# FNet mixing plus MLP on one core: the column transform taken for pairs of row blocks, with seven block products for eight on four fifths of its columns

## The chip, the cores and the metric

The kernel runs on one core of one Trainium2 chip. The metric is the device time of one execution in microseconds, taken as the median of several runs.

## What is computed

The reference, cut to what matters (S = 2048 rows, D = 640 columns, F = 1536 hidden units, all float32):

```python
xn = layernorm(x)                                   # without scale and shift, eps 1e-5
a  = einsum("bsd,ed->bse", xn, dft_hid_re)          # wr in the kernel
b  = einsum("bsd,ed->bse", xn, dft_hid_im)          # wi
y  = einsum("ts,bse->bte", dft_seq_re, a) - einsum("ts,bse->bte", dft_seq_im, b)   # cr, ci
h  = gelu(einsum("bsd,df->bsf", xn, w1) + b1)       # tanh form
return x + y + einsum("bsf,fd->bsd", h, w2) + b2
```

The four transform matrices are inputs like any other; nothing is assumed of them. The kernel takes y in the other order: first the sequence transform, u = cr xn and v = -ci xn, then the column transform, y = u wr' + v wi'.

## The kernel before

TensorE multiplies in float32r. To keep float32 accuracy every operand is held as two forms, a high part (a float32r copy, made on ScalarE, L147) and a low part (what the copy left out, a subtraction on VectorE, L148). `split` makes both. A product of two operands is three matmuls of 128 x 128 by 128 x 512: high by high, high by low, low by high (`product`, L259 to L261).

**First half, the MLP.** Four row blocks of 512 rows (t = 0 to 3), each with 12 steps (i = 0 to 11) over chunks of 128 hidden units. At step i TensorE computes `hidden` for the step after next (15 matmuls), ScalarE takes its gelu and the high form, VectorE the low form (`gelu`, into `hs`), and then `output` multiplies the `hs` made two steps ago into five PSUM banks (15 matmuls). `background(t, i)` runs ahead of that in the program, so its instructions stand ahead of the step's gelu on ScalarE, VectorE and SyncE. It prepares the next row block's layer norm: at i = 4 (t = 1, 2; at t = 0 two steps later) the scaled rows go to DRAM in 16 transfers (`xs`), four transfers bring them back in another order (`load_z`), and at t = 1 three more load rows of x. It also prepares the forms of wr and wi in t = 1 and 2: `load_w` brings a column chunk (`wraw`), `prep_w` turns it on VectorE, splits it and stores the two forms to DRAM (`wts`), one of the ten chunks at each odd i. In t = 3 the operands of the sequence transform are built.

**Second half, the transforms.** `blocks` lists eight stages, four row blocks for each half of the rows summed over; the second half has the order 3, 0, 1, 2. The sequence transform of a stage is done with seven block products for eight: `windows` gives seven products (w) with two entries each (u = 0, 1), 216 matmuls in all, into the PSUM banks X, Y, Z (two each), US and VS. `form(n + 3)` makes the moving operand of the entry after next but one, in one of three buffers `as`, so that ScalarE's copy waits until TensorE has finished the buffer's old entry. `beside` lists for each entry what stands on the other engines beside it: turns of loaded pieces of cr and ci (`turn`), sums of them (`f3`, `f5`, `f6`, `f7`) and gathering of finished banks into `sums` (`gather`). The sums of the first half of the rows wait in DRAM (`parts1`, `parts2`).

Behind each of the last four stages stands the column transform of that row block: ten chunks (five of wr, five of wi) by five output blocks by three matmuls, 150 in all. The weights' forms come from DRAM through three buffers (`load_ws`, `ws`), the sums are split as moving operands (`split_uv`, `uv`), and the result is turned on VectorE, added to the residual and MLP rows (`add_block`) and stored (`store`).

The order on each engine is that of the program (a manual schedule). All loads and stores go through SyncE's queue, but the last stage's stores, of which ScalarE's queue takes half. Transfers wait in that queue for whatever stands ahead of them.

## Time and profile before

| | |
|---|---|
| time, median of 3 runs | 875.88 us (875.66 to 876.95) |
| the profiled execution's own time | 875.63 us |
| its span, first to last instruction | 873.9 us |
| granted TensorE clock, mean | 0.998 |
| TensorE busy | 866.0 us, 3814 matmuls |
| VectorE busy | 560.1 us |
| ScalarE busy | 303.8 us |
| DMA | 149.70 MB, mean 171 GB/s |

In the lines of the profile L12 is line 12 of the kernel. PE is TensorE, PEld its weight load, DVE VectorE, ACT ScalarE, SP SyncE; SPq and ACTq are transfers issued by SyncE and ScalarE. A timeline line has start, duration, engine, source line, operation, output<-input, and in brackets how long the engine was idle before and what ended that. A group's line has its busy time and mean in ns, and then idle time before it. A window's line has the length, the busy time of PE, PEld, DVE, ACT and POOL with instructions in brackets, the granted clock, the DMA share and GB/s.

### The profile page before, as it was taken

Reading aid. Unit: us, or ns where it says so; the run is one execution under the profiler, and the core shown is the slowest. Engines: PE = TensorE matmul, PEld = TensorE weight load, DVE = VectorE, ACT = ScalarE, POOL = GpSimd, SP = SyncE. Lnnn points to the kernel's source line nnn. Section 1 sums busy time; section 2 is a strip of 40 time slices with the busy share of each in tenths; the row PEclk is TensorE's granted clock in tenths of the full one; section 3 lists DMA queues with packets and bytes.
Section 4 is the critical chain, followed back from the end, with each engine's and each line's share of the span. In section 5 each row is a group of like instructions: output and inputs, shape, how many; then the busy total and the mean of one; then the engine's idle time right before and its main releaser. Section 6 shows DMA issues by size and latency. Waiting matters only on the chain.

```text
span 873.9 us, 10010 instructions
## 1 busy us (share of the span) xinstructions
PE 866.0 (99%) x3814; PEld 715.5 (82%) x3814; DVE 560.1 (64%) x700; ACT 303.8 (35%) x409; POOL 21.0 (2%) x22
## 2 busy tenths in 40 slices
PE   9999999999999999999999999999999999999997
PEld 7888888888888888878888888888888888888886
DVE  6554542535243778989888888884687379737713
ACT  5454432334233655433434343331133113302310
POOL 0000300030003000000000000000000000000000
PEclk9999999999999999999999999999999999999999
DMA  6746368535736967959544499628773959247603
GB/s 180 225 133 171 76 165 205 132 98 139 165 91 172 365 269 136 203 115 227 120 148 110 134 268 268 204 49 254 193 237 90 268 160 267 86 162 265 240 0 61
DMA packets 166527, 149.70 MB, mean 171 GB/s; under 512 B 44240, under 2 KB 145104, under 8 KB 165200
## 3 DMA queue, kind: packets, MB, share of 16 engines
q1 hardware_dynamic: 160528, 147.10, 61.7%
q10 hardware_dynamic: 5952, 1.97, 0.9%
q8 instruction: 30, 0.49, 0.2%
q14 instruction: 17, 0.14, 0.1%
HBM read 111.29 MB, written 37.75 MB: 171 GB/s over the span
## 4 chain that ended last, share of the span: by engine, by line
PE 98%; DVE 1%; ACT 0%; issue 0%; DVEq 0%
PE banks L259 26%; PE banks L260 26%; PE banks L261 26%; PE banks L277 19%; PE banks L523 1%; PE banks L544 0%; DVE as L148 0%; DVE v L421 0%; DVE u L421 0%; ACT as L147 0%; DVE yo L421 0%; DVE yt_last L987 0%; ACT xt L147 0%; DVE zeros L514 0%; DVE r L398 0%
## 5 line engine op out<-in xcount | busy, mean ns | idle before, releaser
L147 ACT ACTIVATE as<-r 128x1024 fp32r<-128x1024 f32 x80 | 85.0, 1063 | 212.5 <-PE banks L261 187.7
L259 PE MATMUL banks<-as,xab 128*128 128x512 f32 x352 | 136.9, 389 | 0.0
L260 PE MATMUL banks<-as,xab 128*128 128x512 f32 x352 | 136.9, 389 | 0.0
L261 PE MATMUL banks<-as,xab 128*128 128x512 f32 x352 | 136.9, 389 | 0.0
L148 DVE TENSOR_TENSOR as<-r,as 128x1024 fp32r<-128x1024 f32 x80 | 97.2, 1216 | 43.3 <-ACT as L147 43.2
L292 DVE TENSOR_TENSOR hs<-ab,hs 128x512 fp32r<-128x512 f32 x48 | 36.5, 760 | 109.3 <-ACT hs L290 109.3
L277 PE MATMUL banks<-xt,xab 128*128 128x512 f32 x420 | 99.2, 390 | 0.2 <-ACT xt L147 0.2
L277 PEld LDWEIGHTS banks<-xt,xab 128*128 128x128 f32 x420 | 78.5, 188 | 17.2 <-ACT xt L147 1.3
L259 PE MATMUL banks<-as,xc 128*128 128x512 f32 x224 | 87.3, 390 | 0.4 <-DVE v L421 0.4
L261 PE MATMUL banks<-as,xc 128*128 128x512 f32 x224 | 87.2, 389 | 0.0
L260 PE MATMUL banks<-as,xc 128*128 128x512 f32 x224 | 87.1, 389 | 0.0
L259 PEld LDWEIGHTS banks<-as,xab 128*128 128x128 f32 x352 | 66.1, 188 | 13.7
L261 PEld LDWEIGHTS banks<-as,xab 128*128 128x128 f32 x352 | 66.1, 188 | 13.7
L260 PEld LDWEIGHTS banks<-as,xab 128*128 128x128 f32 x352 | 66.1, 188 | 13.7
L286 ACT ACTIVATE ab<-banks,b1c 128x512 f32<-128x512 f32 x48 | 33.0, 687 | 115.9 <-PE banks L277 115.7
L259 PE MATMUL banks<-uv,ws 128*128 128x512 f32 x165 | 64.3, 389 | 0.0
L260 PE MATMUL banks<-uv,ws 128*128 128x512 f32 x165 | 64.2, 389 | 0.0
L261 PE MATMUL banks<-uv,ws 128*128 128x512 f32 x165 | 64.2, 389 | 0.0
L147 ACT ACTIVATE as<-rt 128x1024 fp32r<-128x1024 f32 x32 | 34.0, 1062 | 70.5 <-PE banks L261 59.8
L277 PE MATMUL banks<-xt,as 128*128 128x512 f32 x240 | 57.0, 389 | 0.0
L277 PEld LDWEIGHTS banks<-xt,as 128*128 128x128 f32 x240 | 45.1, 188 | 9.3
L259 PEld LDWEIGHTS banks<-as,xc 128*128 128x128 f32 x224 | 42.0, 188 | 9.5 <-DVE v L421 0.8
(131 smaller groups left out, 1334.9 us busy)
## 6 DMA issues: line engine op xcount, KB each, us to landing
ws<-wts SPq DMA_DIRECT2D x33, 640.0 KB, 5.5
raw<-in_A_dft_seq_re_dram SPq DMA_DIRECT2D x64, 256.0 KB, 5.8
raw<-in_A_dft_seq_im_dram SPq DMA_DIRECT2D x64, 256.0 KB, 5.3
wts<-wst SPq DMA_DIRECT2D x10, 640.0 KB, 3.2
xs<-x SPq DMA_DIRECT2D x64, 80.0 KB, 1.8
xo<-in_A_x_dram SPq DMA_DIRECT2D x16, 320.0 KB, 6.4
forms_ab<-xab SPq DMA_DIRECT2D x4, 1280.0 KB, 5.8
x<-in_A_x_dram SPq DMA_DIRECT2D x14, 320.0 KB, 6.0
```

The costliest lines, as they stand in the source:

```text
L147: nc.scalar.activation(h, s, AF.Copy)
L148: nc.vector.tensor_tensor(l, s, h.bitcast(F32), op=ALU.subtract)
L259: nc.tensor.matmul(acc, wh, mh, start=first, stop=False, skip_group_check=goes_on)
L260: nc.tensor.matmul(acc, wh, ml, start=False, stop=False, skip_group_check=goes_on)
L261: nc.tensor.matmul(acc, wl, mh, start=False, stop=last, skip_group_check=goes_on)
L277: nc.tensor.matmul(acc, W1[i][:, a, j * P : (j + 1) * P], XT[j][:, b], start=n == 0, stop=n == len(steps) - 1)
L286: nc.scalar.activation(a, acc, AF.Gelu_apprx_tanh, bias=b1c[:, i : i + 1])
L292: nc.vector.tensor_tensor(hs[:, 1], a, hs[:, 0].bitcast(F32), op=ALU.subtract)
L523: nc.tensor.matmul(wacc, warm[:, :P], warm, start=True, stop=True)
```

## The change

The column transform is done for two row blocks at once. The stages of the second half of the rows are taken as two pairs (blocks 3 and 0, then 1 and 2): sequence transform of the first (`s`), of the second (`s`), then one column transform for both (`y`). Over a pair, (u, v) of two blocks is a 2 by 2 array of blocks, and wr and wi by two pairs of output blocks another; their product is formed with seven block products for eight. The fifth output block (every chunk of the fifth 32 columns of a quarter) is outside this array; it rides as a third column on four of the seven products. So the products have widths of 3, 3, 3, 2, 2, 2, 3 blocks of 128 (`GWIDE`), each over five chunks.

The sums of wr and wi that this needs are made in t = 1 and 2 of the MLP half: `prep_w(s)` takes a chunk j of both matrices in four steps (k = 0 to 3), turns them (`turn_w`), adds and subtracts, and `put_w` splits and stores seven forms (`wits`) through two buffers `wst`. The sums of the row blocks (t1 to t4 below) are made on VectorE beside the matmuls; to hold two blocks, `sums` has two sets. The operands of the `y` entries go through the same three `as` buffers as those of `s` (three entries for each product, of two, two and one chunks); the weights' forms come through five places in the first pair and nineteen in the second (`open_g`, `load_g`). The `v` and `v1` sums of the first block of a pair are gathered at its last entry. In the second pair finished columns are stored as they come, half of the transfers from ScalarE's queue.

The diff, cut to its core:

```diff
-    wts = dram.tile([2 * ND, P, 2, D], F32, name="wts")
...
+    GWIDE = (3, 3, 3, 2, 2, 2, 3)
+    wits = [dram.tile([ND, P, 2, n * P], F32, name=f"wit{w}") for w, n in enumerate(GWIDE)]
...
+    def turn_w(m, j):
...
+        nc.vector.transpose(
+            t.rearrange("p (c q i) -> p q c i", q=Q, i=B),
+            A.pop(("wraw", m)).rearrange("p (q c) i -> p q c i", q=Q),
+        )
...
+    def put_w(w, j, main, odd=None, negative=False):
+        n = GWIDE[w] * P
+        t = A["w"].tile([P, 2, 3 * P], F32R, tag="wst", bufs=2, name=f"wst{w}_{j}")
+        split(t[:, 0, : 2 * P], t[:, 1, : 2 * P], main)
+        if odd is not None and not negative:
+            split(t[:, 0, 2 * P :], t[:, 1, 2 * P :], odd)
+        elif odd is not None:
+            h, l = t[:, 0, 2 * P :], t[:, 1, 2 * P :]
+            nc.scalar.activation(h, odd, AF.Copy, scale=-1.0)
+            nc.vector.scalar_tensor_tensor(l, odd, -1.0, h.bitcast(F32), op0=ALU.mult, op1=ALU.subtract)
+        nc.sync.dma_start(wits[w][j], t[:, :, :n].bitcast(F32))
+    def prep_w(s):
+        if s == 0:
+            load_w(0, 0)
+            load_w(1, 0)
+        j, k = divmod(s - 1, 4)
+        if s == 0 or j >= ND:
+            return
+        if k == 0:
+            turn_w(0, j)
+            turn_w(1, j)
+            if j + 1 < ND:
+                load_w(0, j + 1)
+                load_w(1, j + 1)
+        (r1, r2, r4), (i1, i2, i4) = (
+            (A["wt", m][:, : 2 * P], A["wt", m][:, 2 * P : 4 * P], A["wt", m][:, 4 * P :]) for m in range(2)
+        )
+        if k == 1:
+            put_w(0, j, r1, r4)
+            put_w(1, j, i1, i4)
+            add(r4, r4, i4)
+        if k == 2:
+            put_w(6, j, i2, i4, True)
+            add(i2, i2, r2)
+            put_w(2, j, i2, r4)
+            add(r2, r1, r2, ALU.subtract)
+        if k == 3:
+            add(r1, i2, r1, ALU.subtract)
+            put_w(3, j, r1)
+            add(i1, i1, r1, ALU.subtract)
+            put_w(4, j, i1)
+            put_w(5, j, r2)
...
-    windows = [(h, t, w) for h, t in blocks for w in range(NW)]
+    stages = []
+    for k, blk in enumerate(blocks):
+        stages.append(("s", blk))
+        if k >= NT and (k - NT) % 2:
+            stages.append(("y", (blocks[k - 1][1], blk[1])))
+    entries = [(*st, w, u) for st in stages for w in range(NW) for u in range(2 if st[0] == "s" else 3)]
...
+    KU, KV = ("u1", "u2", "u"), ("v1", "v2", "v")
+    MOV = ((KU, 0), (KV, 0), (KU, 1), (KU, 1), (KV, 1), (KU, 0), (KV, 0))
...
     def form(n):
-        if n >= 2 * len(windows):
+        if n >= len(entries):
             return
-        src = held(SRC[n // 2 % NW], n % 2)
+        kind, what, w, u = entries[n]
         a = A["as"][:, n % 3]
-        split(a[:, 0], a[:, 1], src)
-    def add(dst, a, b, op=ALU.add):
-        nc.vector.tensor_tensor(dst, a, b, op=op)
+        if kind == "s":
+            split(a[:, 0], a[:, 1], held(SRC[w], u))
+        else:
+            names, which = MOV[w]
+            src = sums[what[which], names[u]]
+            if u < 2:
+                split(a[:, 0], a[:, 1], src)
+            else:
+                split(a[:, 0, 0], a[:, 1, 0], src)
...
-            if i < 2 * ND:
-                if i == 0:
-                    load_w(m, 0)
-                if i % 2 == 1:
-                    prep_w(m, i // 2)
-                elif i // 2 + 1 < ND:
-                    load_w(m, i // 2 + 1)
+            prep_w((t - 1) * NF + i)
...
+    sets = {(0, t): int(t < NT - 1) for t in range(NT)}
+    sets.update({blk: (0, 1, 1, 0)[p] for p, blk in enumerate(blocks[NT:])})
...
+    def new_sum(h, t, k):
+        shape = (P, 2, TB) if k in PAIRS else (P, TB)
+        sums[t, k] = fr_tile(shape, f"{k}_{sets[h, t]}", f"{k}_{h}_{t}")
+        return sums[t, k]
...
+        ahead = p == 2
+        direct = h == 0 or p in (0, 2)
+        second = p in (1, 3)
+        def t1(k):
+            if not second:
+                return lambda: None
+            ua, ub = sums[blocks[b - 1][1], KU[k]], sums[t, KU[k]]
+            return lambda: add(ub, ub, ua, ALU.subtract)
...
-                4: [uv(0)] if h else [],
+                4: [t1(0)] if second else [],
...
+                6: [t1(2)] if second else [],
...
+                12: [t1(1)] if second else [],
...
+            if second and n == 3:
+                A["g", b] = [A["ws"][:, k] for k in range(3)]
+            if second and 3 <= n < 6:
+                post.append(lambda: load_g(b, n - 3))
...
+            if n == 6 and second:
+                def load_y4():
+                    yo[t, 4] = A["y4"](f"y4_{t}")
+                    nc.sync.dma_start(yo[t, 4], ys[t][:, :, 4 * B :])
+                post.append(load_y4)
+            if n == 11 and p == 3:
+                post += [lambda: open_g(b), lambda: [load_g(b, i) for i in range(3, len(A["g", b]))]]
+            if n == 13 and p == 1:
+                post += [lambda: open_g(b), lambda: [load_g(b, i) for i in range(3, len(A["g", b]))]]
+            if n == 13 and direct:
+                post += [g("v", vs, op=ALU.subtract), g("v1", x_), lambda: f5(0), lambda: f5(1)]
...
+    def open_g(b):
+        last = b == len(blocks) - 1
+        for k in ("b", "a") if last else ("b",):
+            r = A["raw"].tile([P, 16 * P], F32R, tag=f"raw_{k}", bufs=1, name=f"gr_{k}{b}")
+            A["g", b] += [r[:, i * 6 * P : (i + 1) * 6 * P] for i in range(2)]
+        if last:
+            for c in range(NK):
+                r = A["xab", c].rearrange("p a b -> p (a b)")
+                A["g", b] += [r[:, i * 6 * P : (i + 1) * 6 * P] for i in range(3)]
+    def load_g(b, i):
+        if i >= NW * ND:
+            return
+        w, c = G[i]
+        n = GWIDE[w] * P
+        places = A["g", b]
+        g = places[i % len(places)][:, : 2 * n].rearrange("p (a b) -> p a b", a=2)
+        GT[b, i] = g
+        nc.sync.dma_start(g.bitcast(F32), wits[w][c])
...
+        def t2(k):
+            return lambda: add(s(1, KU[k]), s(1, KV[k]), s(1, KU[k]), ALU.subtract)
+        def t3(k):
+            return lambda: add(s(0, KU[k]), s(1, KU[k]), s(0, KU[k]), ALU.subtract)
+        def t4(k):
+            return lambda: add(s(0, KV[k]), s(0, KV[k]), s(1, KU[k]), ALU.subtract)
+        def columns(k):
+            return s(1, ("u1", "u2")[k]).rearrange("p a b -> p (a b)").rearrange("p (n e) -> p n e", n=NB)
+        def load_yb():
+            for k in range(2):
+                nc.sync.dma_start(columns(k), ys[tb][:, :, 2 * k * B : 2 * (k + 1) * B])
...
+        def out_a(c0, c1):
+            return lambda: store(ta, ya[:, :, c0:c1], c0, c1, True) if last else None
+        def odd():
+            yt = turned(us, f"yo_{tb}")
+            add_turned(ya[:, :, 4 * B :], yt)
+            add_turned(yo[tb, 4], yt)
+            out_a(4 * B, DQ)()
...
+        pre = {
+            17: [lambda: add(s(1, "v1"), s(1, "v1"), x_)],
+        }.get(n, [])
+        post = {
+            0: [lambda: gather(1, tb, "v1", z_), lambda: gather(1, tb, "v", vs, op=ALU.subtract), f5s[0]],
+            1: [f5s[1]],
+            3: [to(ya[:, :, : 2 * B], x_, f"ya1_{ta}")],
+            4: [t2(0)],
+            5: [t2(1)],
+            6: [to(ya[:, :, : 2 * B], y_, f"ya2_{ta}", out_a(0, 2 * B)), t2(2)],
+            7: [odd],
+            8: [t3(0)],
+            9: [copy(s(1, "v1"), z_), t3(1)],
+            10: [t3(2)],
+            11: [t4(0)],
+            12: [copy(s(1, "v2"), x_), t4(1)],
+            13: [t4(2)],
+            14: [load_yb],
+            15: [lambda: add(s(1, "v2"), s(1, "v2"), z_)],
+            16: [to(columns(0), s(1, "v2"), f"yb1_{tb}", lambda: store(tb, columns(0), 0, 2 * B, last))],
+            18: [to(columns(1), s(1, "v1"), f"yb2_{tb}", lambda: store(tb, columns(1), 2 * B, 4 * B, last))],
+            19: [f6s[0]],
+            20: [f6s[1], to(yo[tb, 4], vs, f"yb4_{tb}", lambda: store(tb, yo[tb, 4], 4 * B, DQ, last))],
+        }.get(n, [])
+        if not last:
+            if n == 10:
+                loads[:] = steps_of_load(put_off[0])
+            if 10 <= n < 14:
+                post.append(loads[n - 10])
+            if n == 18:
+                post.append(lambda: load_part(blocks[b + 1][1], "u"))
+            if n == 20:
+                post.append(lambda: load_part(blocks[b + 1][1], "u1"))
+                post.append(lambda: load_a(put_off[1]))
+                def end():
+                    to(ya[:, :, 2 * B : 4 * B], x_, f"ya3_{ta}")()
+                    store(ta, ya, 0, DQ)
+                later.append(end)
+        return pre, post
...
+    def hidden_entry(n, b, w, u):
+        last = b == len(blocks) - 1
+        where = (X, Y, Z, X, Z, X, X)[w]
+        def use_g(acc, j, pos, first, stop, goes_on=False):
+            r, k = (n - u + (pos // 2)) % 3, pos % 2
+            a = A["as"][:, r]
+            use(acc, GT[b, w * ND + pos], j, a, k, first, stop, goes_on)
+        def wide(j, pos):
+            use_g(bank(where + j), j, pos, w < 3 and pos == 0, pos == ND - 1, w > 2)
+        mine = (2 * u, 2 * u + 1) if u < 2 else (4,)
+        if w == 6 and last:
+            if u == 0:
+                for pos in range(ND):
+                    use_g(bank(VS), 2, pos, False, pos == ND - 1)
+                for pos in range(ND):
+                    wide(0, pos)
+            elif u == 1:
+                for pos in range(ND):
+                    wide(1, pos)
+            return
+        if w == 6 and u == 0:
+            for pos in range(4):
+                use_g(bank(VS), 2, pos, False, False)
+        for pos in mine:
+            for j in range(2):
+                wide(j, pos)
+        for pos in mine:
+            if w < 2:
+                use_g(bank(US), 2, pos, w == 0 and pos == 0, w == 1 and pos == ND - 1)
+            if w == 2:
+                use_g(bank(VS), 2, pos, pos == 0, False)
+            if w == 6 and u == 2:
+                use_g(bank(VS), 2, pos, False, True)
+        for pos in mine:
+            load_g(b, w * ND + pos + len(A["g", b]))
...
+            w, u = entries[n][2:]
+            if kind == "s":
+                sequence_entry(n, what, w, u)
+                pre, post = beside(*what, n - first)
+            else:
+                hidden_entry(n, b, w, u)
+                pre, post = hidden_beside(b, n - first)
+            for f in later:
+                f()
+            later.clear()
+            for f in pre:
+                f()
+            form(n + 3)
+            for f in post:
+                f()
+        first += count
```

`sequence_entry` holds the matmuls of the old loop over `windows`. In a pair ta is its first block and tb its second; u1, u2, u (KU) and v1, v2, v (KV) are the sums of a block for its five chunks.

More of the change, by code (lines that the diff above doesn't have):

```diff
@@ L602, in background @@
         if t in (1, 2):
-            m = t - 1
             if t == 1 and i == 0:
@@ L940, in hid @@
-        def hid(k, i):
-            cols = slice(i * P, (i + 1) * P)
-            product(
-                acc[i],
-                (WS[t, k][:, 0, cols], WS[t, k][:, 1, cols]),
-                (UV[k][:, 0], UV[k][:, 1]),
-                k == 0,
-                k == NV - 1,
-            )
-        x_ = banks[:, X : X + 2]
-        more = {k: [] for k in range(NV)}
-        more[0].append(lambda: gather(1, t, "v", bank(VS), op=ALU.subtract))
-        more[4].append(lambda: gather(1, t, "v1", x_))
@@ new lines @@
+    first = 0
+    for kind, what in stages:
+        b = blocks.index(what) if kind == "s" else b
+        count = NW * (2 if kind == "s" else 3)
+        for n in range(first, first + count):
+            w, u = entries[n][2:]
+            if kind == "s":
+                sequence_entry(n, what, w, u)
+                pre, post = beside(*what, n - first)
+            else:
+                hidden_entry(n, b, w, u)
[9 more added lines that the diff above has]
+        first += count
+        if n + 1 < len(entries):
+            X, Y, Z = Y, Z, X
+        if kind == "y":
+            put_off.clear()
@@ new lines @@
+    t = blocks[-2][1]
+    y = yo[t]
+    add_turned(y[:, :, 2 * B : 3 * B], turned(bank(X), "yt_2"))
+    store(t, y[:, :, 2 * B : 3 * B], 2 * B, 3 * B, True)
+    yt = A["yt"]("yt_last")[:, 0].rearrange("p (n i) -> p n i", i=B)
+    d, a = y[:, :, 3 * B : 4 * B], bank(X + 1).rearrange("p (n i) -> p n i", i=B)
+    for n0 in (0, NB // 2):
+        rows_ = slice(n0, n0 + NB // 2)
+        nc.vector.transpose(yt[:, rows_], a[:, rows_])
+        add(d[:, rows_], d[:, rows_], yt[:, rows_])
+        store(t, d, 3 * B, 4 * B, True, n0, n0 + NB // 2)
```

176 lines of the change are left out of this document (65 added, 111 removed).

## The prediction

> **What bounds the kernel now.** I read the chain that ended last first, then the busy times in windows, then the timelines of SyncE's queue and ScalarE around the places that the change touches.
>
> ```profile
> PE 866.0 (99%) x3814; PEld 715.5 (82%) x3814; DVE 560.1 (64%) x700; ACT 303.8 (35%) x409; POOL 21.0 (2%) x22
> ...
> PE 98%; DVE 1%; ACT 0%; issue 0%; DVEq 0%
> ...
> 102.05 3.40 PE banks L277 x15
> ...
> 20.00:345.00 325.00, 325.00 (x1435) 269.19 (x1435) 162.32 (x292) 134.00 (x217) 20.24 (x15) 1.00 0.62 169
> 386.00:440.00 54.00, 54.00 (x240) 44.71 (x239) 46.34 (x43) 21.87 (x23) 0.00 (x0) 1.00 0.73 171
> PE banks L259 <- DVE v L421: 0.4, 1, 0.4
> ```
>
> The first line gives busy time, share and instructions of each engine. The second is the chain by engine: TensorE is 98% of it. The third is a piece of the chain: 15 matmuls in 3.40 us, 0.2267 us each, one every time the last has streamed. The two windows (us, then busy time of PE, PEld, DVE, ACT, POOL, then clock, DMA share, GB/s) show PE busy for all 325 us of the MLP half while VectorE works 162, and in a stage of the sequence transform for all 54 us while VectorE works 46.3. The last line is the only wait for data that PE has in the sequence half, 0.4 us. So a matmul taken away is worth 0.2267 us, and any wait of PE that the change brings is paid in full. VectorE has half its time free in the MLP half, but only a seventh in the other.
>
> **What is removed.** The column transform takes 10 chunks x 5 output blocks x 3 matmuls = 150 for a row block, 600 for four. After it is 7 products of widths 3, 3, 3, 2, 2, 2, 3 = 18, x 5 chunks x 3 = 270 for a pair, 540 for two. Gone: 60 matmuls x 0.2267 = **-13.6 us**.
>
> **Its forms, made in the MLP half.** Now 55 ScalarE copies and 90 VectorE instructions for 10 and 20. By time they lie in VectorE's free half. By order they don't. ScalarE is one queue, and it also runs the gelus that PE needs two steps later. Step k = 3 of a column chunk stores three forms through two buffers, so the third copy (of wit5) waits until the store of the first (wit3) has landed. For chunks 0 and 3 this step falls on i = 4 of t = 1 and t = 2, where the layer norm queues its transfers on SyncE just ahead. Here is before at t = 1, then t = 2:
>
> ```profile
> 130.35 8.10 SPq L190 DMA_DIRECT2D xs<-x  x16
> 140.05 1.91 SPq L216 DMA_DIRECT2D z<-xs  x4
> 142.00 1.47 SPq L165 DMA_DIRECT2D x<-in_A_x_dram  x3
> 143.51 6.75 SPq L330 DMA_DIRECT2D wraw<-in_A_dft_hid_re_dram  x4
> wraw<-in_A_dft_hid_re_dram SPq DMA_DIRECT2D x1, 80.0 KB, 7.5
> 220.75 1.91 SPq L216 DMA_DIRECT2D z<-xs  x4
> 222.71 6.35 SPq L330 DMA_DIRECT2D wraw<-in_A_dft_hid_im_dram  x4
> wraw<-in_A_dft_hid_im_dram SPq DMA_DIRECT2D x1, 80.0 KB, 7.0
> 132.69 0.69 ACT L286 ACTIVATE ab<-banks,b1c 128x512 f32<-128x512 f32 x1 [2.53 <-PE banks L277]
> 146.29 0.69 ACT L286 ACTIVATE ab<-banks,b1c 128x512 f32<-128x512 f32 x1 [5.45 <-PE banks L277]
> 227.89 0.69 ACT L286 ACTIVATE ab<-banks,b1c 128x512 f32<-128x512 f32 x1 [5.45 <-PE banks L277]
> 128.87 1.28 ACT L286 ACT_TABLE_LOAD   x1
> 147.01 0.63 ACT L290 ACTIVATE hs<-ab 128x512 fp32r<-128x512 f32 x1
> 147.68 0.69 DVE L292 TENSOR_TENSOR hs<-ab,hs 128x512 fp32r<-128x512 f32 x1 [6.11 <-ACT hs L290]
> L476 ACT ACTIVATE xab<-sums 128x256 fp32r<-128x256 f32 x8 | 3.3, 419 | 0.0
> 154.07 0.74 ACT L147 ACTIVATE wst<-wt 128x640 fp32r<-128x640 f32 x1 [6.43 <-DMA wts<-wst]
> wts<-wst SPq DMA_DIRECT2D x10, 640.0 KB, 3.2
> ```
>
> The first transfer behind z and x is a wraw load of 80 KB, issued at 143.51. It lands 7.5 us later, at 151.0, since everything ahead has to pass first. In the new order the store of wit3 stands in exactly this place. So ScalarE's copy of wit5 starts at 151.0 for a gelu that could have run at 132.69. Behind it on ScalarE: the copy 0.42, the table load 1.28 (in before done early, now behind the copy), gelu 0.69, its copy 0.63, with gaps 3.05, so hs at 154.05; VectorE's low half 0.69 later. PE wants this hs when the hidden product two steps on has ended, at 146.29. PE waits 7.8 us, and 0.45 again for the low half: 8.2. At t = 2 no x loads follow z: 222.71 + 7.0 = 229.7, hs at 232.75 against 227.89, 4.9 + 0.45 = 5.3. Together **+13.5 us**. (The wait is not new in kind: in before ScalarE stood 6.43 us for such a store at i = 7, but no gelu was late, so nothing showed.) Least, if a store lands in the median 3.2 us of the last row: 3.9 + 1.5 = 5.4; most, with backlog from t = 2's i = 0, where a store stands behind ys<-xo: 15.5. I take 13.5; the row is for the same place in the queue. The other three steps of this kind (i = 8, 0, 8) have no such queue, or end inside the 13.6 us from gelu to use.
>
> **The clock after such a stop.**
>
> ```profile
> 868.00:869.00 1.00, 0.49 (x3) 0.07 (x1) 0.45 (x1) 0.00 (x0) 0.00 (x0) 1.00 0.90 147
> 870.00:871.00 1.00, 0.00 (x0) 0.00 (x0) 0.26 (x1) 0.00 (x0) 0.00 (x0) 0.94 0.55 90
> 871.00:872.00 1.00, 0.00 (x0) 0.00 (x0) 0.00 (x0) 0.00 (x0) 0.00 (x0) 0.50 0.84 133
> 1.92 8.71 PE banks L523 x26
> ```
>
> PE's last matmul ends at 868.5; at 870.9 the granted clock falls to 0.5. So idle of 2.4 us is enough, at least once. The price of coming back: the 26 warm-up matmuls took 8.71 us for 26 x 0.2267 = 5.9, that is 2.8 lost. Two stops, 0 to 2.8 each; I take 2.0 each, nearer the one row there is, **+4.0**. [...]
>
> **The pair stages.** Two stages of 270 matmuls, 61.2 us, take the place of four of 34. What is tight lies on two short stretches.
>
> ```profile
> L148 DVE TENSOR_TENSOR as<-r,as 128x1024 fp32r<-128x1024 f32 x80 | 97.2, 1216 | 43.3 <-ACT as L147 43.2
> L147 ACT ACTIVATE as<-r 128x1024 fp32r<-128x1024 f32 x80 | 85.0, 1063 | 212.5 <-PE banks L261 187.7
> L421 DVE TENSOR_TENSOR v<-v,banks 128x1024 f32<-128x1024 f32 x16 | 19.5, 1216 | 2.0 <-PE banks L261 1.6
> L748 ACTq DMA_DIRECT2D out_dram<-yo x10: 373/434/533, 861.8 to 870.9; - x10
> ws<-wts SPq DMA_DIRECT2D x33, 640.0 KB, 5.5
> 142.00:143.00 1.00, 1.00 (x6) 0.83 (x5) 0.00 (x0) 0.00 (x0) 0.00 (x0) 1.00 1.19 293
> 145.00:146.00 1.00, 1.00 (x6) 0.84 (x5) 0.00 (x0) 0.00 (x0) 0.00 (x0) 1.00 1.20 213
> 148.00:149.00 1.00, 1.00 (x6) 0.84 (x5) 0.37 (x1) 0.00 (x0) 0.00 (x0) 1.00 1.04 407
> ```
>
> Last pair, entry 12 (counted from the end of entry 6). Its finished columns are stored from ScalarE's queue too, so ScalarE waits for VectorE. VectorE: low half 2.35, transpose and add of ya2 to 4.75; ScalarE: two issues of 0.43 to 5.65, form of entry 10 to 6.7; VectorE: low half to 7.95, the odd column to 9.3; ScalarE: two more issues to 10.2, forms 11 and 12 to 11.8; VectorE: low halves and a sum to 13.8; ScalarE's copy of the accumulator Z 1.06, to 14.9. PE wants Z again after 4.08 + 2.04 + 2.72 + 2.72 + 1.36 = 12.9: **+2.0**. In the first pair nothing is stored there and it fits.
>
> Entry 18, from the end of entry 16: copy 1.1, low half to 2.3, transpose and add of yb1 to 4.7, and only then the sum that frees X, to 5.9. In the last pair two issues hold ScalarE to 5.5, so the form for entry 20, which the same accumulator takes last, comes at 6.2 (high) and 6.9 (low), wanted at 1.36 + 2.72 = 4.1: **+2.6**. In the first pair VectorE alone gives 5.9 - 4.1 = 1.8, but there transfers are later: five places hold the forms, so product 7's pieces are issued as product 6 ends, behind a raw piece (0.5 MB of it), 0.5 MB of ys in 256-byte rows and product 6's own 1.3 MB. With product 7's first four, 1.6 MB, that is 3.9 MB to land within 12.2 us of entry 12's end, or 320 GB/s. The rates while the queue was full in before were 213 to 293 under z's 640-byte rows and up to 407 under x's 2560-byte rows. The mix here has both. At 407 the pieces come in time and VectorE's 1.8 is left; at 300 they need 13 us and 1 for the landing, about 2 late; at 250, 4.4. Each product of this stage that starts late also issues its later pieces late, so I take the middle of 2 and 4.4, **+3.2**. The last pair has 19 places, loaded ahead.
>
> Other edits at nothing: the added sums (t1 to t4) and f5, v gathers in blocks beside 49 us of matmuls (forms stand three entries ahead, and before's tightest place cost 0.4): 0 to 1.5. Product 1's late pieces, whose buffer VectorE frees at the block's end: 0 to 1.5. The tail is as before, two half transposes and their stores.
>
> **Sum.** -13.6 + 13.5 + 4.0 + 2.0 + 2.6 + 3.2 = +11.7, on the profiled execution's 875.63 (span 873.9, 1.7 around it): **887.3 us**. The median of the runs shown is 875.88, 0.25 more, which I leave aside; 0.2%, what a measurement of this kernel can tell from no change, is 1.75.
>
> **The rivals.**
> 1. Transfers pass each other: the wit3 store lands 3.2 us after its issue whatever is ahead, and product 7's pieces arrive in time. Then the stops are 3.9 and 1.5, at most one loses clock (0 here), and the first pair pays 1.8: -13.6 + 5.4 + 2.0 + 2.6 + 1.8 = -1.8, **873.8**, faster. It decides at a landing 4.1 us after the issue: above that the two stops cost over 7.2 and nothing of the 13.6 is left. For it: 3.2 is the median of ten stores. Against it: the 80 KB load that took 7.5. [...] No run here shows a store in that place.
> 2. Same, but the clock pays 2.8 and the first pair 3.2: 873.8 + 2.8 + 1.4 = **878.0**.
> 3. Transfers are slower: the pair stage's pieces at 213 GB/s also miss products 5 and 6 (1.3 MB in 6.8 us is 193 with nothing else), 3 us twice; stops 15.5; clock 5.6: 887.3 + 6 + 2 + 1.6 = **896.9**. For it: the raw and ys loads share these microseconds. Against: ws at 640 KB in 5.5 us kept up.
> 4. The change saves no matmul time: no; the built program has 3754 matmuls for 3814.
>
> **How the numbers follow.** Forecast 0.70, rival 1 0.08, rival 2 0.10, rival 3 0.12, rival 4 nothing. The forecast's own bounds are 881 (no clock loss, 11.5 of stops) to 892 (clock 5.6, 4.4, small edits 1.5). The range leaves out rival 1 and the far end of rival 3: **877 to 896**. Faster by over 0.2%: 0.07, rival 1 but for a little of it; within: 0.05, the rest of rival 1 and the low side of rival 2; slower: 0.88.
>
> **What would show it.** Right: in the timeline of ScalarE two waits of wst for the DMA of wit3, some 13 to 16 us each, at i = 4 of t = 1 and 2; PE idle behind them, before matmuls that take hs; granted clock 0.5 at their ends; in the last pair gaps at entries 12 and 18. Wrong: PE without gaps from 20 us to the sequence half (then 13.5 + 4.0 fall away), or gaps there of 2 us and less; PE gaps in products 3 to 5 of the first pair (rival 3); a first pair without a gap at product 7.

## The result, and the profile after

The changed kernel takes **901.43 us** (median of 4 runs, 900.25 to 903.15) against 875.77 us for the kernel before beside it: a ratio of 1.0292 (95% interval 1.0272 to 1.0311). The forecast was 887.3 with a range to 896. The sign was right, and the size was not: +25.7 us against +11.7. The profiled execution took 900.25 us, with a span of 898.5.

The page of the changed kernel, engines and chain:

```profile
PE 862.9 (96%) x3754; PEld 707.9 (79%) x3754; DVE 623.3 (69%) x792; ACT 332.2 (37%) x460; POOL 20.9 (2%) x22
...
PE 75%; DVE 8%; DMA 8%; ACT 3%; SPq 2%; issue 2%; POOL 0%; ACTq 0%; DVEq 0%; POOLq 0%
```

The longest waits of its PE but for the start (line, what it waited for: us in total, times, longest):

```profile
PE banks L269 <- ACT hs L300: 18.1, 2, 9.9
PE banks L269 <- DMA ws<-wit: 3.8, 1, 3.8
PE banks L269 <- ACT as L157: 2.5, 1, 2.5
...
PE banks L269 <- ACT v L1055: 1.9, 1, 1.9
```

The 60 matmuls are gone (3754 for 3814). PE's busy time shrinks by 3.1 us and not by 13.6, for the most part because a matmul at half clock holds PE for longer (0.427 us from start to start behind entry 18, for 0.2267). The chain is 75% PE, no longer 98%. The waits name the places: two for `hs` behind a gelu (the stops in the MLP half), one for pieces of the weights' forms (first pair, product 7), one for the form of an entry (last pair, entry 18), one for the copy `v` of an accumulator (last pair, entry 12).

Its timeline: SyncE's queue at the first stop, t = 1, then what ScalarE did, then both at t = 2:

```profile
130.90 8.83 SPq L200 DMA_DIRECT2D xs<-x  x16
141.16 1.91 SPq L226 DMA_DIRECT2D z<-xs  x4
143.11 1.45 SPq L175 DMA_DIRECT2D x<-in_A_x_dram  x3
144.92 9.58 SPq L361 DMA_DIRECT2D wit<-wst  x3
153.09 0.42 ACT L157 ACTIVATE wst<-wt 128x256 fp32r<-128x256 f32 x1 [18.61 <-DMA wit<-wst]
153.52 1.28 ACT L296 ACT_TABLE_LOAD   x1
154.82 0.69 ACT L296 ACTIVATE ab<-banks,b1c 128x512 f32<-128x512 f32 x1
155.54 0.63 ACT L300 ACTIVATE hs<-ab 128x512 fp32r<-128x512 f32 x1
...
235.62 2.20 SPq L226 DMA_DIRECT2D z<-xs  x4
237.86 1.18 SPq L361 DMA_DIRECT2D wit<-wst  x2
245.28 0.42 ACT L157 ACTIVATE wst<-wt 128x256 fp32r<-128x256 f32 x1 [15.02 <-DMA wit<-wst]
```

The stores in its transfers from 143 to 153 and from 236 to 246 us (KB each, median us from issue to landing):

```profile
wit<-wst SPq DMA_DIRECT2D x2, 256.0 KB, 8.0
wit<-wst SPq DMA_DIRECT2D x2, 256.0 KB, 7.4
```

The order is the forecast one: `xs`, `z`, `x`, then three stores, and ScalarE's third copy stands for the first of them. Behind the copy come the table load, the gelu and its high form, which ends at 156.2 (155.54 + 0.63).

Windows of the changed kernel (length, busy time of PE, PEld, DVE, ACT, POOL, then granted clock, DMA share, GB/s): a clear stretch of the MLP half, the two stops, then product 7 of the first pair and entries 12 and 18 of the last.

```profile
20.00:140.00 120.00, 120.00 (x531) 99.36 (x530) 60.40 (x116) 48.65 (x80) 6.73 (x5) 1.00 0.61 158
148.00:161.00 13.00, 4.78 (x12) 3.54 (x13) 5.14 (x11) 6.66 (x12) 0.00 (x0) 0.61 0.57 162
240.00:253.00 13.00, 4.81 (x13) 3.40 (x12) 4.97 (x11) 6.66 (x12) 0.00 (x0) 0.61 0.46 122
...
706.00:718.00 12.00, 8.18 (x30) 6.28 (x29) 7.70 (x7) 2.13 (x3) 0.00 (x0) 0.86 1.07 295
860.00:866.00 6.00, 3.87 (x16) 2.51 (x15) 4.62 (x5) 3.88 (x5) 0.00 (x0) 1.00 0.65 172
880.00:888.00 8.00, 5.36 (x17) 3.78 (x16) 7.17 (x8) 0.63 (x1) 0.00 (x0) 0.79 0.32 74
```

A clock of 0.61 over 13 us is 10.2 us at a half (10.2 x 0.5 + 2.8 = 7.9 of 13). By the same step the 0.86 and 0.79 are 3.4 us at a half each.

From here on, the **loss** of a place is the sum over its matmuls of the time from one start to the next start, less 0.2267. It holds gaps and slow clock alike. From 20 us to the last matmul it was 0.6 us before the change; now it is 39.0:

| place | predicted | measured |
|---|---|---|
| stop at t = 1: the wait | 8.2 | 10.1 |
| stop at t = 2: the wait | 5.3 | 8.4 |
| clock behind the two | 4.0 | 4.5 (2.2 each) |
| last pair, entry 12 | 2.0 | 2.8 (the gap 2.1) |
| last pair, entry 18 | 2.6 | 4.6 (the gap 2.6) |
| first pair, product 7 | 3.2 | 5.7 (the gap 4.0) |
| small edits | 0 | 2.3 (1.4 of it in the sequence stage between the column stages, 0.6 and 0.4 at products 1 and 6 of the first pair) |
| matmuls gone | -13.6 | -13.6 |
| sum | +11.7 | +24.8; the end behind the last matmul is 0.2 shorter, so +24.6, as by the profiled executions |

### The profile page after: what moved, and what is told of

Its sections match the earlier page's. It is cut to its first block, busy times and chain, and to the rows that moved or that the text cites. A ratio compares the mean times of both kernels' runs of the same rounds, so it can differ in the third digit from the quotient of the medians.

```text
span 898.5 us, 10232 instructions
## 1 busy us (share of the span) xinstructions
PE 862.9 (96%) x3754; PEld 707.9 (79%) x3754; DVE 623.3 (69%) x792; ACT 332.2 (37%) x460; POOL 20.9 (2%) x22
## 4 chain that ended last, share of the span: by engine, by line
PE 75%; DVE 8%; DMA 8%; ACT 3%; SPq 2%; issue 2%; POOL 0%; ACTq 0%; DVEq 0%; POOLq 0%
PE banks L269 21%; PE banks L270 21%; PE banks L271 21%; PE banks L287 12%; DMA wit<-wst 4%; DVE as L158 1%; ACT wst L157 1%; ACT as L157 1%; DMA w1r<-in_B_w_dram 1%; DMA xo<-in_A_x_dram 1%; SPq L200 1%; DVE u L398 1%; DMA ws<-wit 1%; DMA raw<-in_A_dft_seq_re_dram 1%; DVE wst L158 1%
## 5 line engine op out<-in xcount | busy, mean ns | idle before, releaser
L269 PE MATMUL banks<-as,xab 128*128 128x512 f32 x407 | 159.1, 391 | 2.8 <-ACT as L157 2.5
L270 PE MATMUL banks<-as,xab 128*128 128x512 f32 x407 | 159.3, 391 | 0.2 <-DVE as L158 0.2
L271 PE MATMUL banks<-as,xab 128*128 128x512 f32 x407 | 158.9, 390 | 0.0
L269 PEld LDWEIGHTS banks<-as,xab 128*128 128x128 f32 x407 | 76.7, 188 | 19.6 <-ACT as L157 2.9
L270 PEld LDWEIGHTS banks<-as,xab 128*128 128x128 f32 x407 | 76.8, 189 | 17.1 <-DVE as L158 1.2
L271 PEld LDWEIGHTS banks<-as,xab 128*128 128x128 f32 x407 | 76.8, 189 | 15.8
L269 PE MATMUL banks<-hs,xc 128*128 128x512 f32 x120 | 48.5, 404 | 18.1 <-ACT hs L300 18.1
L158 DVE TENSOR_TENSOR wst<-wt,wst 128x256 fp32r<-128x256 f32 (+1 forms) x50 | 17.3, 380 | 59.0 <-ACT wst L157 59.0
L157 ACT ACTIVATE wst<-wt 128x256 fp32r<-128x256 f32 (+1 forms) x50 | 17.5, 379 | 87.8 <-DMA wit<-wst 56.6
```

The costliest lines, as they stand in the source:

```text
L157: nc.scalar.activation(h, s, AF.Copy)
L158: nc.vector.tensor_tensor(l, s, h.bitcast(F32), op=ALU.subtract)
L269: nc.tensor.matmul(acc, wh, mh, start=first, stop=False, skip_group_check=goes_on)
L270: nc.tensor.matmul(acc, wh, ml, start=False, stop=False, skip_group_check=goes_on)
L271: nc.tensor.matmul(acc, wl, mh, start=False, stop=last, skip_group_check=goes_on)
```

## The experiments

All were compared with the kernel before on the same chip. The median of the kernel before was 876.87 beside the four runs on ScalarE's queue, ys, SyncE's stores and late transposes, 876.10 beside the last two, and 876.08 beside the rest. The expectations reckon from 901.2 for the change; the median shown above is 0.2 more. A loss in a run is read from its one profiled execution.

**The stores in another queue.** One word is changed:

```diff
     def put_w(...):
...
-        nc.sync.dma_start(wits[w][j], t[:, :, :n].bitcast(F32))
+        nc.scalar.dma_start(wits[w][j], t[:, :, :n].bitcast(F32))
```

> One edit to the changed kernel: the 35 stores of the forms of wr and wi are issued from ScalarE's queue instead of SyncE's, so that none stands behind the layer norm's transfers. Theory (the two stops of TensorE in the MLP half are ScalarE's wait for a buffer whose store is queued behind xs, z and x): both stops go, 12.3 and 10.5 us of the changed kernel's trace with the slow clock behind them, so 901.2 - 22.8 = 878.4, less than 1 us of new gaps from the 35 issues on ScalarE. Rival (ScalarE and VectorE have too much to do there, 55 copies and 90 instructions, whatever the order): the stops stay or grow, 900 or more.

Measured: 885.8 us (881.54 to 888.18), ratio 1.0097 (1.0063 to 1.0132). PE runs without loss from 20 to 186 us and from 212 to 380, so both stops are gone. But the time is 7.4 us over the expected 878.4. New gaps of less than 1 us were expected; 6.7 come up at the boundary of the row blocks t = 1 and 2, in two stops: 2.2 us at 188 and 4.4 at 203. ScalarE's timeline at the second of them, in which the third store of i = 0 of t = 2 is to be made:

```profile
196.35 0.52 ACTq L361 DMA_DIRECT2D wit<-wst  x1
202.26 0.42 ACT L157 ACTIVATE wst<-wt 128x256 fp32r<-128x256 f32 x1 [6.39 <-DMA wit<-wst]
```

ScalarE stands 6.39 us for a landing again, and PE's longest wait there is for `hs`, 2.0.

At the boundary the store of the row block's results (`ys`), the load of its residual rows (`xo`) and a load of x go out in the same microseconds as the stores of the forms. The place in the queue was the cause at i = 4. That those transfers are what delays the stores at the boundary is argued from the order, not shown.

**The forms ahead of the layer norm.** The order alone is changed; the stores stay in SyncE's queue:

```diff
     def background(t, i):
+        if t in (1, 2):
+            ...
+            prep_w((t - 1) * NF + i)
         if t + 1 < NT:
             ...
-        if t in (1, 2):
-            ...
-            prep_w((t - 1) * NF + i)
```

> Only the order in the MLP half is changed: the step of the forms stands ahead of the layer norm's part of the same step on every engine, no longer behind it. Theory (the stops at i = 4 of t = 1 and 2 come from three stores that stand behind the layer norm's transfers in SyncE's queue): both stops go, 22.8 us of 24.6 lost, and as the stores then delay the loads of residual rows at the end of a row block (as with the stores in ScalarE's queue), 2 to 5 us come up around 175 to 210 us. Time 879 to 884. Rival (the amount of ScalarE's and VectorE's work or of bytes in t = 1 and 2 is what is late, whatever the order): stops of the same 20 us and more somewhere in t = 1 and 2, time over 895.

Measured: 885.12 us (883.07 to 888.32), ratio 1.0111 (1.0088 to 1.0134). Three rows of its windows:

```profile
20.00:165.00 145.00, 145.00 (x641) 120.06 (x640) 67.91 (x134) 57.99 (x98) 6.74 (x5) 1.00 0.64 167
165.00:200.00 35.00, 31.26 (x130) 23.51 (x129) 22.23 (x42) 15.02 (x31) 6.84 (x5) 1.00 0.57 154
200.00:380.00 180.00, 180.00 (x796) 149.05 (x795) 114.54 (x213) 84.98 (x149) 6.74 (x5) 1.00 0.72 200
```

The same work of ScalarE and VectorE and the same bytes, in another order: no loss at either i = 4. 5.9 us come up between 169 and 196 for the 2 to 5 expected, and the time is 1.1 over the range given. Together with the run before it, this shows that the 22.8 us came from where the stores stood, and rules out the amount of work.

**No load of ys.**

```diff
-            14: [load_yb],
+            14: [],
```

This kernel leaves out the residual and MLP part of four fifths of the columns of each pair's second block.

> One edit to the changed kernel: the two loads of ys in 256-byte rows in the pair stages are left out (four fifths of the columns of each pair's second block then lack the residual and MLP part). Theory (in the first pair TensorE waits at product 7 for pieces of the forms that are queued behind these loads): the loss there falls from 5.7 us to 1.8, what VectorE's chain alone gives, and the clock does not fall; the last pair, whose pieces are loaded ahead, stays at 2.7 and 4.6; 901.2 - 3.9 = 897.3. Rival (VectorE's chain of yb1 and the sum that frees X is the whole of it): 5.7 stays, 901.

Measured: 898.74 us (896.49 to 901.63), ratio 1.0252 (1.0226 to 1.0278). Product 7 of the first pair loses 1.8 for 5.7, as expected, and the clock does not fall there. But product 6 ahead of it now loses 2.0 for 0.4, so the two together go from 6.1 to 3.8. The waits of PE in this stretch:

```profile
PE banks L269 <- DVE v L398: 1.1, 1, 1.1
PE banks L269 <- DMA ws<-wit: 1.0, 2, 0.6
```

At product 7 it is VectorE's sum that frees the accumulator X that is late, as forecast. The late pieces, 1.0 in all, are those of product 6. How the load of ys delayed product 7's pieces stands in SyncE's queue, first in the changed kernel, then without ys:

```profile
702.74 4.70 SPq L1052 DMA_DIRECT2D u<-ys  x2
707.53 2.58 SPq L1023 DMA_DIRECT2D ws<-wit  x3
...
703.55 3.80 SPq L1023 DMA_DIRECT2D ws<-wit  x3
```

SyncE takes 4.7 us to issue the two loads, and only then issues product 7's first piece: 5.2 us after product 6 has begun, for 1.7 without ys. From issue to landing the three pieces take the same median in both runs, 5.4 us. So they came late by their issue and not by a slower transfer. Whether the issue of ys is slow of itself or waits for room in the queue is not shown.

**Stores of the last pair from SyncE alone.**

```diff
-            return lambda: store(ta, ya[:, :, c0:c1], c0, c1, True) if last else None
+            return lambda: store(ta, ya[:, :, c0:c1], c0, c1) if last else None
...
-            16: [to(columns(0), ..., lambda: store(tb, columns(0), 0, 2 * B, last))],
+            16: [to(columns(0), ..., lambda: store(tb, columns(0), 0, 2 * B))],
```

> One edit to the changed kernel: in the last pair the stores of the first block's finished columns and of yb1 are issued from SyncE alone, none from ScalarE. Theory (ScalarE stands before those stores until VectorE has added, and its forms and its copy of Z come late): the gap at entry 12 goes (2.7 us), the one at entry 18 loses about the half of its 4.6 (VectorE's chain stays), 901.2 - 5.0 = 896.2. Rival (VectorE simply has too much in these entries): both gaps stay within 0.5 us, 901.

Measured: 898.47 us (897.71 to 902.37), ratio 1.0262 (1.0233 to 1.0291). Entry 12 loses nothing (2.8 before), so ScalarE's issues were all of it. Entry 18 keeps 4.1 of 4.6, where about half was expected to go, and PE's wait there is now for VectorE's low form:

```profile
PE banks L270 <- DVE as L158: 2.3, 1, 2.3
```

Here the prediction's picture was incomplete: with ScalarE free, VectorE's own order is nearly as late (a gap of 2.4 us for 2.6). The end, from the last matmul's start to the end of the span, takes 6.9 for 5.5, so a part of what entry 12 gave is lost there.

**The transposes into yb later.**

```diff
-            16: [to(columns(0), s(1, "v2"), f"yb1_{tb}", ...)],
-            18: [to(columns(1), s(1, "v1"), f"yb2_{tb}", ...)],
-            19: [f6s[0]],
+            18: [to(columns(0), s(1, "v2"), f"yb1_{tb}", ...)],
+            19: [f6s[0], to(columns(1), s(1, "v1"), f"yb2_{tb}", ...)],
```

> One edit to the changed kernel: the turns and sums of yb1 and yb2 stand two and one entries later on VectorE, behind the sum that frees X; the transfers keep their order. Theory (two different causes at product 7): in the last pair, where VectorE's chain is the cause, the gap at entry 18 goes (4.6 us); in the first pair, where the pieces come late, at least 4 of 5.7 stay; some 1 to 2 us come back in the block behind it, whose first forms stand behind yb2 now: 901.2 - 4.6 + 0.5 = 897. Rival (one cause for both, VectorE): both go, 891. Rival (one cause for both, transfers): both stay, 901.

Measured: 901.03 us (899.83 to 904.56), ratio 1.0283 (1.0257 to 1.0309): nothing won in all, though entry 18 loses 0.2 for 4.6. The gain was given back in four places. Products 5 to 7 of the first pair lose 6.9 for 6.1. The sequence stage behind them loses 3.4 for 1.4. The end takes 7.4 for 5.5. And the clock fell behind entry 12, which it had not done in the changed kernel:

```profile
864.00:866.00 2.00, 0.66 (x3) 0.19 (x1) 2.00 (x3) 0.52 (x1) 0.00 (x0) 1.00 0.81 318
866.00:867.00 1.00, 0.44 (x1) 0.38 (x2) 0.59 (x1) 1.00 (x2) 0.00 (x0) 0.86 0.03 12
867.00:870.00 3.00, 3.00 (x8) 2.32 (x7) 2.52 (x4) 0.97 (x2) 0.00 (x0) 0.50 0.00 0
```

Eight matmuls in 3 us, for 13 at 0.2267 each, are about half speed. Entry 12 loses 4.4 for 2.8, with the same gap of 2.06. The edit moves the stores of yb1 and yb2 along with the transposes, so by itself it doesn't tell the two apart; the run with SyncE's stores does that for yb1.

**The pair stages alone, three edits together.**

```diff
-            return lambda: store(ta, ya[:, :, c0:c1], c0, c1, True) if last else None
+            return lambda: store(ta, ya[:, :, c0:c1], c0, c1) if last else None
...
-            14: [load_yb],
+            14: [load_yb] if last else [],
+            17: [] if last else [load_yb],
...
```

and the transposes at 18 and 19 as above.

> Only the pair stages are changed: finished columns of the first block are stored from SyncE alone, the transposes into yb1 and yb2 stand two and one entries later, and in the first pair the load of ys stands at entry 17, behind the issues of product 7's pieces. Theory (product 7 of the first pair has two causes at once, the load of ys ahead of the pieces and VectorE's transposes ahead of the sum that frees X, so that taking one away leaves the other): the first pair's loss goes from 5.7 to 1 or less, entry 12 of the last pair from 2.7 to 0, entry 18 from 4.6 to 0.2, together 12 us less than after: 888 to 891. Rival (product 7 waits for its pieces behind the 1.3 MB of product 6 themselves): 2 us and more stay in the first pair, 891 to 893.

Measured: 891.82 us (890.44 to 895.07), ratio 1.0184 (1.0166 to 1.0202). The last pair loses 0.1 for 7.4. Product 7 of the first pair loses 0.9 for 5.7, as the theory of two causes has it. But product 6 loses 1.9 for 0.4, by late pieces (ws<-wit 1.4 in all), so that 2.8 are left in the stretch, as much as in the rival, though one product earlier than it said, and the time lies in the rival's range. The sequence stage behind loses 3.5 for 1.4, and the end takes 7.6 for 5.5.

**The forms' steps at other places.** With the pair stages as in the run just told:

```diff
+    PLAN = {0: [0], 1: [1], 2: [2], 3: [3], 5: [4, 5], 6: [6], 7: [7], 8: [8], 9: [9], 13: [10], 14: [11], 15: [12, 13], 17: [14], 18: [15], 19: [16, 17], 20: [18], 21: [19], 22: [20]}
     def background(t, i):
...
-            prep_w((t - 1) * NF + i)
+            for s_ in PLAN.get((t - 1) * NF + i, ()):
+                prep_w(s_)
```

> The change, with the pair stages as in the run with those alone, and the forms' steps put at other places in t = 1 and 2: none at i = 4, 10 and 11 of t = 1, nor at i = 0 and 4 of t = 2 and i = 11; two steps together at i = 5 of t = 1 and i = 3 and 7 of t = 2, one of each two being the turn without stores. Theory (no matter is left but the place of the stores in the queue): no stop over 1 us in the MLP half, 60 matmuls gone, some 3 us left over in all: 864 to 869, faster than before. Rival (the transfers of the forms delay the layer norm's or the residual rows' in any place): stops of 3 us and more around 175 to 210 or 270 us, 870 to 877.

Measured: 878.73 us (875.94 to 879.84), ratio 1.0027 (1.0018 to 1.0037). This misses the 864 to 869, and lies above the rival's 877 too. The stops of i = 4 are gone, but 2.5 us come at 153, 1.2 at 177 and 4.5 at 273 (some 1.7 of them slow clock). That is the rival's picture.

> As the run before this one (same places), with the forms' step ahead of the layer norm's part of each step. Theory: as there, 863 to 868; ahead of the layer norm the stores wait for less, so that it is at most 1 us from the other. Rival: the layer norm's four transfers of z come later behind the stores and the hidden products of the next row block wait for them, 870 and over.

The same with the forms ahead of the layer norm. Measured: 877.31 us (875.55 to 878.59), ratio 1.0012 (1.0003 to 1.0021), not the 863 to 868. 1.3 us at 153, 1.1 at 176, 4.2 at 272. The last of these, by what stands in SyncE's queue (i = 10 of t = 2), what GpSimd and VectorE wait for, and PE's longest wait from 265 to 285 us:

```profile
259.13 3.85 SPq L361 DMA_DIRECT2D wit<-wst  x3
263.03 2.26 SPq L319 DMA_DIRECT2D xo<-in_A_x_dram  x4
271.86 7.09 POOL L328 TENSOR_TENSOR xo<-xo,ot 128x512 f32<-128x512 f32 x5 [79.73 <-DMA xo<-in_A_x_dram]
273.17 0.72 DVE L326 STREAM_TRANSPOSE ot<-banks 128x512 f32<-128x512 f32 x1 [5.56 <-POOL xo L328]
PE banks L269 <- DVE ot L326: 2.2, 2, 1.5
```

Three stores stand ahead of the load of residual rows. GpSimd's adds stand for that load, VectorE's transposes, which empty PE's banks, stand for GpSimd, and PE for them. The rival had the direction, but named the transfers of z.

**No store ahead of that load either.** Steps 4 and 5 are moved from i = 5 to i = 6 of t = 1, and the last ones end at i = 9 of t = 2; in the last pair the transposes stand at entries 17 and 18:

```diff
-    PLAN = {..., 5: [4, 5], 6: [6], 7: [7], 8: [8], 9: [9], ..., 20: [18], 21: [19], 22: [20]}
+    PLAN = {..., 6: [4, 5], 7: [6], 8: [7], 9: [8, 9], ..., 20: [18], 21: [19, 20]}
```

> As the run with the new places and the forms' step first, but with no step at i = 5 of t = 1 and i = 10 of t = 2 either, so that the last three stores are in the queue before the residual rows' load at i = 10, and in the last pair the transposes into yb1 and yb2 one entry earlier (entries 17 and 18). Theory (what is left in the MLP half is again stores ahead of or behind other transfers: 1.4 us at 152, 4.2 us at 272; and the later transposes hold up the last stores, 7.5 us from the last matmul's start to the end for 5.8 before): 152 and 272 lose under 1 us each, the end is 6 us, 871 to 874, faster than before. Rival (the stores delay whatever they meet, in any place): 4 us of stops come up elsewhere in t = 1 and 2, 876 to 879.

Measured: **873.11 us** (870.70 to 874.86), ratio 0.9963 (0.9950 to 0.9975). 152 and 272 lose nothing; 0.8 at 175 and 1.1 at 257 are all of the MLP half. The end is still 7.5 and not 6. SyncE's stores alone lengthened it to 6.9 and late transposes alone to 7.4; which of the two holds it here is not shown. The sequence stage behind the first pair loses 5.1, of which 1.7 is clock that fell behind a gap of 2.3 at 722.

**The parts' load ahead of ys.**

```diff
-            if n == 18:
-                post.append(lambda: load_part(blocks[b + 1][1], "u"))
+            if n == 17:
+                post.insert(0, lambda: load_part(blocks[b + 1][1], "u"))
```

> The same, and the load of the next pair's u parts one entry earlier, ahead of the load of ys in the first pair. Theory: the loss of 1.7 us at 727 (VectorE has stood 4 us for u<-parts there) goes to the 0.4 that it has in the change as given; product 7 of the first pair loses up to 1 us more; 0 to 1.3 us less than the run without. Rival: the sums stand in VectorE's order, not in the queue, and nothing is won: the same time within 0.5 us.

Measured: **871.76 us** (871.19 to 872.64), ratio 0.9950 (0.9938 to 0.9962). The sequence stage loses 3.6 for 5.1 in the run beside it; the 1.7 us of slow clock that are gone are more than this difference. The stretch at 721 keeps 1.4, where 0.4 was expected: VectorE still stands 3.8 us there for u<-parts, so the earlier issue did little. Products 6 and 7 of the first pair lose 0.8 for 2.2, but the edit stands behind the issues of product 6's pieces and can't have helped those. The intervals of the two runs overlap, and what this edit is worth (1.4 us of median) is not shown; that both kernels are faster than before, by less than 1%, is. Its windows of the MLP half in two parts, and of the first pair with the stage behind it:

```profile
20.00:165.00 145.00, 145.00 (x642) 120.09 (x641) 68.45 (x135) 59.15 (x99) 6.75 (x5) 1.00 0.63 165
165.00:380.00 215.00, 213.81 (x937) 175.05 (x936) 139.42 (x256) 100.23 (x180) 13.49 (x10) 1.00 0.70 193
640.00:760.00 120.00, 117.53 (x509) 94.50 (x508) 96.68 (x92) 37.36 (x38) 0.00 (x0) 1.00 0.82 234
```

And a line of ScalarE's timeline:

```profile
152.41 0.42 ACT L157 ACTIVATE wst<-wt 128x256 fp32r<-128x256 f32 x1 [8.80 <-DMA wit<-wst]
```

The clock is full in all three windows. At i = 6 of t = 1 ScalarE still stands 8.8 us for the landing of a store, but TensorE doesn't wait for a gelu behind it: it is busy for 145.00 of the 145.00 us. The same 60 matmuls are gone as in the change, and 4.3 us of their 13.6 are left in the time (876.10 - 871.76).

## Why the prediction was right and wrong

**What was right.** The value of a matmul, the size of the clock loss behind the stops (2.2 each for 2.0), and the place of every term in the sum: the two `hs` waits at i = 4 of t = 1 and 2, the first pair's product 7, entries 12 and 18 of the last pair. No loss in the MLP half is elsewhere. Rival 1 (transfers pass each other) is refuted by stores that landed 8.0 and 7.4 us after their issue, against 7.5 and 7.0 forecast. Rival 3, at 896.9, came nearest in the number, but 6 us of it by luck: products 5 and 6 of the first pair, which were to lose them, lose 0.4 (at 702).

**What failed: the sizes, in five terms.**

1. *The stops, 18.4 for 13.5.* The prediction took the issue time of the store from the trace of before (143.51) and let the layer norm's own transfers stand where they were. In the changed kernel they are later too, since step k = 2 of the forms stands ahead of them on ScalarE and waits for a store itself:

```profile
124.48 0.42 ACT L157 ACTIVATE wst<-wt 128x256 fp32r<-128x256 f32 x1 [3.40 <-DMA wit<-wst]
```

`xs` begins at 130.90 for 130.35, `z` is issued at 141.16 for 140.05, the store at 144.92 for 143.51, and it takes 8.0 for 7.5. (Why the 16 issues of `xs` also take 0.7 us longer is not shown.) The copy that was to start at 151.0 starts at 153.09, 2.1 later, and the wait is 1.9 longer. At t = 2 the same sum moved on by the first stop's 12.3 us gives 242.0 for the copy, which starts at 245.28: 3.3 later, and the wait is 3.1 longer. There the copy of step k = 2 stands 4.8 us for a landing, and `xs` begins 2.4 later than the shifted row. The row was "for the same place in the queue", but the change also moved the place in time. The upper bound of 15.5 for the two stops was passed as well.
2. *Product 7 of the first pair, 5.7 for 3.2.* The wait for the pieces is 3.8, between the 2 and 4.4 of the prediction, but that is luck: the prediction got it from the rate of the transfers (407 to 250 GB/s), and the runs show that the pieces landed as fast as without ys and were issued late, behind 4.7 us of issuing ys. The rest, 1.7, is clock that the prediction charged to the long stops alone. The 1 us that its working adds for the landing is an estimate near what a store alone in the queue shows: the one of `wts` at 124.79 in the kernel before has its first packet 0.8 us after its issue, and lands 0.5 us behind its last.
3. *Entry 18, 4.6 for 2.6.* The gap is the predicted 2.6, in part by luck: the prediction had 1.8 of it from VectorE alone and the rest from ScalarE's two issues, and without an issue of ScalarE for yb1 the gap is still 2.4. Again 3.4 us at half clock stand behind it.
4. *Entry 12, 2.8 for 2.0.* The gap is 2.1; 0.6 is late in product 4 just ahead of it. The run with SyncE's stores shows that ScalarE's issues are the whole of both.
5. *Small edits, 2.3 for 0*, of which 1.4 in the sequence stage behind the first pair, whose entries the change left much as they were. VectorE stands there for the parts of the sums, in this line of its timeline, and then works without a pause past the two places at 746 and 755 where PE is late. That the one follows from the other is read from this order; no run shows it:

```profile
742.52 1.22 DVE L398 TENSOR_TENSOR u<-u,banks 128x1024 f32<-128x1024 f32 x1 [4.16 <-DMA u<-parts]
```

4.9 for the stops, 0.5 for their clock, 2.5, 2.0, 0.8 and 2.3: 13.0, which takes 887.3 to 900.3; less the 0.2 of the shorter end, this is the profiled 900.25 to within 0.2. The range failed with them: the forecast's own upper bound, 892, counted clock at two places, where the trace has it at four, and 1.5 us for the small edits; the 896 came from rival 3.

**What is shown and what is not.** That the stops are a matter of order is shown by two runs that change only the queue or the order. That entry 12 is ScalarE's issues is shown by one run; that entry 18 is VectorE's transposes is shown by that run, which leaves 4.1, and the one with late transposes, which leaves 0.2. That product 7 of the first pair has two causes is shown by three runs: without ys it loses 1.8, with late transposes alone 5.0, with both changed 0.9. Open are four things: why product 6 loses between 0.3 and 2.0 from run to run, and 0.3 to 1.1 in the four kernels that share the first pair of the change; why the sequence stage behind it loses 3.4 and more in all kernels with late transposes; how much of the longer end comes from the transposes; and the small losses around 175 and 257 of the last run.

## What to carry to other kernels

Work that fits by busy time (ScalarE at 37%) is not free: what counts is the moment at which a queue stands for a transfer, and what urgent instruction is behind it. Put new stores where neither a burst of transfers is ahead of them nor an urgent load behind them; here the places of stores, loads and transposes, with the same matmuls, made the difference between 1.029 and 0.995. A transfer also costs the queue its issue: two loads in 256-byte rows held SyncE for 4.7 us, and the piece behind them was issued 3.5 us later than without them. When an operation is priced from a row of the trace before, move that row by what the change itself puts ahead of it, and charge a gap on TensorE with the clock that may follow it: here 1.7 us behind gaps of 2.06, 2.63 and 3.98 us, and nothing behind another of 2.06.

## What the runs showed of the hardware

The granted clock fell behind short gaps of TensorE. In the changed kernel it fell behind one of 3.98 us (product 7 of the first pair) and one of 2.63 (entry 18 of the last), by its windows for 3.4 us at a half each. In the two stops, of 10.1 and 8.4 us, it fell as well, for 10.2 us each. In the run with later transposes it fell behind a gap of 2.06 (entry 12), but not behind the same 2.06 in the changed kernel, whose clock is full in the windows around it:

```profile
860.10:863.51 3.41, 2.32 (x9) 1.24 (x7) 3.03 (x4) 1.33 (x3) 0.00 (x0) 1.00 1.07 279
863.51:866.92 3.41, 2.37 (x10) 1.96 (x11) 2.51 (x3) 2.45 (x3) 0.00 (x0) 1.00 0.05 17
```

So the length of a gap alone does not decide here; what else does is not shown. Each fall behind one of these three short gaps cost about 1.7 us.
